# Retention in single precision: raw queries, keys, values, scores and states in place of products of 16-bit parts

## The chip, the cores and the metric

The kernel runs on one core of a Trainium2 chip. The metric is the device time of one execution in microseconds (us). Five engines take part, each with its own instruction stream: TensorE (PE in the profile, its weight loads are PEld), VectorE (DVE), ScalarE (ACT), GpSimd (POOL) and SyncE (SP), which issues most DMAs.

## The reference, cut to what matters

A retention layer feeds two mixture-of-experts layers. Only the retention is touched by the change.

```python
B, H, S, D = 4, 8, 576, 64                     # q, k, v: [B, H, S, D], float32
scores = np.matmul(q, k.transpose(0, 1, 3, 2)) / np.sqrt(D)
gamma = 1.0 - 2.0 ** (-5.0 - np.arange(H))
rel = pos[:, None] - pos[None, :]
Dmat = np.where(rel >= 0, gamma[:, None, None] ** rel, 0.0)
x = np.matmul(scores * Dmat, v)                # then [B*S, H*D] = [2304, 512]
x = moe(x)       # 4 experts, all of them for every token, 512 -> 1024 -> 512
x = moe2(x)      # 8 experts, the best one for each token
```

## The kernel before, in words

**Arithmetic.** Nearly all products are made from 16-bit floats. A float32 operand is split into a high and a low 16-bit part: ACT writes the scaled high part, DVE (`split`, L164 and L165) or POOL writes what is left. A product is then three matmuls (`TERMS`: high by high, high by low, low by high) that add up in the same place in PSUM.

**Retention.** A sequence of 576 positions is cut in 6 chunks of 96 positions (`C`, `NC`), which makes 24 steps for the 4 batches (`NSTEP`). A step handles all 8 heads, two at a time: heads 2p and 2p+1 use the two 64-row or 64-column halves of the array, for p of 0 to 3.

- `at_load(s)`: SP issues two loads, `qkr` (queries and keys, positions along the free dimension) and `vkr` (values and keys, positions on the partitions).
- `at_split(s)`: the parts. ACT and DVE split the queries and keys (`x2`) and the keys by rows (`k2`); POOL multiplies the values by the decay table (`vs`, L199), ACT and POOL split the product (`v2`, L205 and L206).
- `at_a(s)`: PE makes the scores (`sc`, L217, 24 matmuls: contraction 64, 96 weight columns, 96 moving columns). DVE applies the mask (`pf`, L221); ACT, DVE and POOL split the result (`p2`, L222 and L223). If the chunk isn't the last of its sequence, PE makes the chunk's contribution to the state (`u`, L233, 24 matmuls of 64 moving columns), DVE adds the old state, POOL multiplies by the decay (`sn`, L240, L241), and ACT and DVE split the state (`ss`, L243 and L244).
- `at_b(s)`: PE multiplies scores and values (`xo`, L255, 24 matmuls of 96 moving columns) and, unless the chunk is the first, adds the product of the state before and the queries (again L255, 24 matmuls). DVE scales the result (`xf`, L273), ACT and POOL split it into `xc` (L282, L283), the input of the first layer.
- `at_store(s)`: SP writes `xf`, and every fourth step `xc`, to HBM.

**First layer.** Tokens go in 6 blocks of 384 (`NB`), 4 steps to a block. For expert 0 (`e == 0`) the kernel runs `l1_first` (L431) and `l2` (L534) on block after block. Block 0 is made in the prologue: `l1_part(0, 2)` after the first two steps and `l1_part(2, 4)` after the next two, between the splits of the weights (`w_first`). From then on `at_hook`, called four times in a block, issues the store of the step before, `at_a(s+1)`, `at_b(s)`, `at_split(s+2)` and the load of step s+3. So retention runs one block ahead of the first layer, and step 23 is issued in block 4. The experts 1 to 3 use seven products in place of eight (`l1_mixed`, L460); for the first of them the weights are mixed and split in block 5 of expert 0 (`w_hook`). The second layer streams its weights and ends the kernel.

**What sets the order.** Each engine works through its own list in order. The lists follow the source, but the framework's planner may move an instruction ahead of another that it expects to be later; the groups of 24 matmuls of a step are mostly kept whole. SP's queue is in order too: a DMA that waits for its buffer holds up the ones behind it. `at_raw` has three buffers for each of the two loads and `raw_p` five for raw weights. PSUM has two banks for the scores, and one each for `u` and `xo`.

Of the kernel before, what the change touches and what calls it, by code (L numbers as in the profile page):

```python
# [28 lines left out]
KD = DM // 128  # L29
# [10 lines left out]
PROD = {1: (0, 0), 2: (1, 1), 4: (2, 5), 5: (3, 4), 6: (4, 7), 7: (5, 6), 3: (6, 3)}  # L40
TERMS = ((0, 0), (0, 1), (1, 0))

S_QK = 2.0 ** 6
S_V = 2.0 ** 6
S_X = 2.0 ** 9
S_W = 2.0 ** 8
S_X1 = 2.0 ** 11
# [6 lines left out]
def _consts():  # L54
    gamma = 1.0 - 2.0 ** (-5.0 - np.arange(H))
    i = np.arange(C)
    fa, fb = {}, {}
    m = np.zeros((128, C))
    m[:C] = i[:, None] <= i[None, :]
    fa["mask"] = m  # L60
    g = gamma[:, None] ** i[None, :]
    x = np.zeros((128, KD, C))
    for p in range(KD):
        x[:64, p] = g[2 * p]
        x[64:, p] = g[2 * p + 1]
    fa["xtab"] = x * (D ** -0.5) * S_X / (S_QK * S_QK * S_V)
    v = np.zeros((128, H))
    v[:C] = (gamma[None, :] ** -i[:, None]) * S_V
    fa["vtab"] = v
    gt = np.zeros((128, KD))  # L70
    gt[:64], gt[64:] = gamma[0::2] ** C, gamma[1::2] ** C
    fa["gtab"] = gt
    fb["ident"] = np.eye(128)
    fb["first"] = np.broadcast_to(E2 - np.arange(E2), (128, E2))
    s = np.arange(NSLOT)
    at = np.arange(128)[:, None] - 2 * np.arange(2)[None, :]
    fb["tau"] = 128.0 * np.maximum(at // 2, 0)
    fb["even"] = 1 - at % 2
# [12 lines left out]
    return fa, fb, f16  # L91
# [13 lines left out]
def kernel(  # L105
# [19 lines left out]
    pe, act, dve, pool, sp = nc.tensor, nc.scalar, nc.vector, nc.gpsimd, nc.sync  # L125
# [8 lines left out]
    ps = ctx.enter_context(tc.tile_pool(name="ps", bufs=2, space=PSUM))  # L134
    w_a = ctx.enter_context(tc.tile_pool(name="w_a", bufs=1))

    ka = const.tile([128, ca.shape[1]], F32, name="ka")
    kb = const.tile([128, cb.shape[1]], F32, name="kb")
    k16 = const.tile([128, c16.shape[1]], F16, name="k16")

    def cst(name, *dims):
        t, at = (ka, of_a) if name in of_a else (kb, of_b)
        o, n = at[name]
        a = t[:, o:o + n]
        if len(dims) == 2:
            return a.rearrange("p (a b) -> p a b", a=dims[0])
        return a
# [26 lines left out]


    at_ctx = ExitStack()
    at_raw = at_ctx.enter_context(tc.tile_pool(name="at_raw", bufs=3))
    at_2 = at_ctx.enter_context(tc.tile_pool(name="at_2", bufs=2))
    at_1 = at_ctx.enter_context(tc.tile_pool(name="at_1", bufs=2))
    ps_2 = at_ctx.enter_context(tc.tile_pool(name="ps_2", bufs=2, space=PSUM))  # L180
    ps_1 = at_ctx.enter_context(tc.tile_pool(name="ps_1", bufs=1, space=PSUM))
    raws, spl, pm, st = {}, {}, {}, {}
    xcs, xfs = {}, {}

    def at_load(s):
# [6 lines left out]

    def at_split(s):

        a, t = raws.pop(s)
        x2 = at_2.tile([128, 2, 2, KD, C], F16, name="x2")
        split(a, x2[:, 0], x2[:, 1], S_QK)
        vs = at_1.tile([C, H, D], F32, name="vs")
        pool.tensor_tensor(out=vs, in0=t[:, 0], in1=cst("vtab", H, 1)[:C].to_broadcast([C, H, D]), op=ALU.mult)  # L199
        v2 = at_2.tile([C, 2, H, D], F16, name="v2")  # L200
        k2 = None
        if s % NC < NC - 1:
            k2 = at_2.tile([C, 2, H, D], F16, name="k2")
            split(t[:, 1], k2[:, 0], k2[:, 1], S_QK)
        act.activation(out=v2[:, 0], in_=vs, func=ACTF.Copy)  # L205
        pool.tensor_tensor(out=v2[:, 1], in0=vs, in1=v2[:, 0], op=ALU.subtract)  # L206
        spl[s] = x2, v2, k2

    def at_a(s):
        x2, v2, k2 = spl[s]  # L210
        p2 = at_2.tile([C, 2, 2, KD, C], F16, name="p2")
        sc = [ps_2.tile([C, KD, C], F32, tag="sc", name="sc") for _ in range(2)]
        for p in range(KD):
            for n, (x, y) in enumerate(TERMS):
                for r in range(2):
# [12 lines left out]
        u = ps_1.tile([128, KD, D], F32, tag="u", name="u")
        for p in range(KD):
            for n, (x, y) in enumerate(TERMS):  # L230
                for r in range(2):
                    h = 2 * p + r
                    pe.matmul(u[64 * r:64 * r + 64, p], lhsT=k2[:, x, h], rhs=v2[:, y, h], start=(n == 0), stop=(n == 2))  # L233
        sn = at_2.tile([128, KD, D], F32, name="sn")
        gt = cst("gtab", KD, 1).to_broadcast([128, KD, D])
        if c == 0:
            dve.tensor_tensor(out=sn, in0=u, in1=gt, op=ALU.mult)
        else:
            so = st[s - 1][0]
            dve.tensor_tensor(out=sn, in0=u, in1=so, op=ALU.add)  # L240
            pool.tensor_tensor(out=sn, in0=sn, in1=gt, op=ALU.mult)  # L241
        ss = at_2.tile([128, 2, KD, D], F16, name="ss", bufs=3)
        act.activation(out=ss[:, 0], in_=sn, func=ACTF.Copy)  # L243
        dve.tensor_tensor(out=ss[:, 1], in0=sn, in1=ss[:, 0], op=ALU.subtract)  # L244
        st[s] = sn, ss

    def at_b(s):
        x2, v2, k2 = spl.pop(s)
        p2 = pm.pop(s)
        c = s % NC  # L250
        o = ps_1.tile([128, KD, C], F32, tag="xo", name="xo")
# [12 lines left out]
        if c:
            ss = st[s - 1][1]
            for p in range(KD):
                for n, (x, y) in enumerate(TERMS):
                    for r in range(2):
                        row = slice(64 * r, 64 * r + 64)
                        into(r, p, ss[row, x, p], x2[row, y, 0, p], 3 + n, n == 2)  # L270
# [12 lines left out]
        pace["pool"] = pool.tensor_tensor(out=lo, in0=xf, in1=hi, op=ALU.subtract)  # L283
        xfs[s] = xf
# [754 lines left out]
    for e in range(E1):  # L1039
        for b in range(NB):  # L1040
# [161 lines left out]
```

## Time and profile before

| | |
|---|---|
| median of 3 runs | 1085.55 us (1085.05 to 1086.11) |
| the profiled execution's own time | 1084.43 us |
| its span, first to last instruction | 1082.7 us |
| mean granted clock of TensorE | 0.991 |
| PE busy in the span | 1032.4 us (95%) |
| DVE, ACT, POOL busy | 536.4, 414.5, 289.3 us |

The page gives each engine's busy time and the groups of instructions; a matmul's shown duration includes its way through the array, so 24 overlapped matmuls show as one merged entry, and the distance from the start of one group to the start of the next is what they cost. What matters is in which stretch an engine is the one that others wait for.

### The profile page before, as it was taken

The numbers are of one execution on the slowest core, as the hardware profiler recorded it, in microseconds if no ns is written. First come the engines' busy times: TensorE is split into PE (matmuls) and PEld (weight loads), VectorE is DVE, ScalarE is ACT, GpSimd is POOL, SyncE is SP. The second block draws the span as 40 slices with busy tenths as digits, with TensorE's granted clock in tenths as the row PEclk, the third lists the DMA queues.
The fourth block names the chain that finished last, engine by engine and source line by source line (L and its number), as shares of the span: only waits on it lengthen the run. The fifth ranks groups of instructions, "written<-read, shape, count | busy, mean of one in ns | idle before, by whom it ended". The sixth has DMA issues, their size and how long they took to land.

```text
span 1082.7 us, 24429 instructions
## 1 busy us (share of the span) xinstructions
PE 1032.4 (95%) x10355; PEld 713.8 (66%) x10355; DVE 536.4 (50%) x1037; ACT 414.5 (38%) x821; POOL 289.3 (27%) x298
## 2 busy tenths in 40 slices
PE   4799999999899999999999999999999999999996
PEld 3665555555466777777666677776677677777674
DVE  5975555753646555544656654645555511111111
ACT  5654445533524444433444444423333122222121
POOL 5655645634643342000211000000001111212121
PEclk9889999999999999999999999999999999999998
DMA  9564333211534545666687676445525253381692
GB/s 271 184 213 132 116 110 95 90 38 60 188 124 158 191 164 216 250 223 210 230 285 280 236 253 218 159 182 207 198 89 197 88 195 126 135 341 60 253 391 93
DMA packets 51314, 196.27 MB, mean 181 GB/s; under 512 B 6510, under 2 KB 14334, under 8 KB 48896
## 3 DMA queue, kind: packets, MB, share of 16 engines
q1 hardware_dynamic: 40336, 150.72, 39.5%
q0 software_dynamic: 10864, 43.94, 11.9%
q8 instruction: 83, 1.36, 0.5%
q14 instruction: 31, 0.25, 0.1%
HBM read 184.76 MB, written 56.53 MB: 223 GB/s over the span
## 4 chain that ended last, share of the span: by engine, by line
PE 45%; issue 11%; DMA 10%; DVE 6%; ACT 1%; POOL 0%; POOLq 0%; SPq 0%; DVEq 0%; ACTq 0%
PE po L534 25%; DMA out_dram<-y_s,sidxm 8%; PE ph L460 8%; PE pq L460 5%; PE py L460 5%; DVE ht L419 2%; DVE s L165 1%; DMA out_dram<-y_s,sidxe 1%; PE tp L597 1%; PE pg L608 1%; DMA w2d<-s 0%; DVE s L505 0%; DVE w L165 0%; PE p_y L892 0%; ACT ht L418 0%
## 5 line engine op out<-in xcount | busy, mean ns | idle before, releaser
L534 PE MATMUL po<-w,ht 128*128 128x512 f16 x1728 | 384.4, 380 | 7.5 <-DVE ht L419 3.9
L534 PEld LDWEIGHTS <-ht 128*128 128x128 f16 x1728 | 167.2, 98 | 205.3 <-DVE ht L419 7.9
L460 PEld LDWEIGHTS <-w 128*128 128x128 f16 x3024 | 249.2, 98 | 5.6 <-issue 1.2
L460 PE MATMUL ph<-xc,w 128*128 128x192 f16 x1296 | 119.1, 246 | 1.0 <-ACT py L484 1.0
L875 PEld LDWEIGHTS <-lane 128*128 128x128 f16 x1920 | 109.0, 98 | 5.1 <-issue 0.9
L875 PE MATMUL p_h<-x_s,lane 128*128 128x128 f16 x1920 | 111.5, 219 | 0.4 <-issue 0.4
L431 PE MATMUL ph<-xc,w 128*128 128x384 f16 (+1 forms) x672 | 103.6, 312 | 8.5 <-DVE ht L419 4.1
L892 PE MATMUL p_y<-lane,h_s 128*128 128x512 f16 x480 | 107.2, 379 | 0.8 <-DVE h_s L885 0.8
L885 DVE SCALAR_TENSOR_TENSOR h_s<-p_h,h_s 128x512 f16<-128x512 f32 x40 | 27.6, 691 | 159.1 <-ACT h_s L884 159.1
L165 DVE SCALAR_TENSOR_TENSOR s<-sr,s 128x512 f16<-128x512 f32 x128 | 88.7, 735 | 22.7 <-ACT s L164 22.6
L546 DVE SCALAR_TENSOR_TENSOR acc<-po,p_sb,acc 128x512 f32<-128x512 f32 x54 | 40.4, 748 | 117.3 <-PE po L534 117.3
L431 PEld LDWEIGHTS <-w 128*128 128x128 f16 x672 | 65.0, 101 | 42.6 <-issue 10.3
L164 ACT ACTIVATE s<-sr 128x512 f16<-128x512 f32 x128 | 72.4, 623 | 35.9 <-DMA sr<-in_w2s_dram 13.4
L892 PEld LDWEIGHTS <-h_s 128*128 128x128 f16 x480 | 46.6, 98 | 52.6 <-DVE h_s L885 1.2
L460 PE MATMUL pq<-xc,w 128*128 128x192 f16 x864 | 79.8, 246 | 0.0
L460 PE MATMUL py<-xc,w 128*128 128x192 f16 x864 | 77.2, 246 | 0.0
L299 POOL DMA_DIRECT2D xc<-xcd x17 | 12.5, 737 | 206.2 <-PE py L460 206.2
L165 DVE SCALAR_TENSOR_TENSOR w<-wr,w 128x512 f16<-128x512 f32 x82 | 61.7, 767 | 10.7 <-ACT w L164 10.6
L484 ACT ACTIVATE py<-ph 128x384 f32<-128x384 f32 x36 | 17.1, 476 | 130.1 <-PE ph L460 130.1
L372 POOL TENSOR_TENSOR wr<-wr 128x512 f32<-128x512 f32 x24 | 34.8, 1450 | 86.4 <-DVE w L165 85.7
L164 ACT ACTIVATE w<-wr 128x512 f16<-128x512 f32 x82 | 49.3, 623 | 19.1 <-DMA wr<-in_w_dram 13.0
L895 POOL DMA_INDIRECT out_dram<-y_s,sidxm x17 | 17.3, 1017 | 146.8 <-ACT y_s L894 138.2
(168 smaller groups left out, 1093.8 us busy)
## 6 DMA issues: line engine op xcount, KB each, us to landing
lane<-w1d SPq DMA_DIRECT2D x20, 2048.0 KB
lane<-w2d SPq DMA_DIRECT2D x20, 2048.0 KB
wr<-in_w_dram SPq DMA_DIRECT2D x32, 512.0 KB
sr<-in_w1s_dram SPq DMA_DIRECT2D x32, 512.0 KB
w1d<-s SPq DMA_DIRECT2D x32, 512.0 KB
sr<-in_w2s_dram SPq DMA_DIRECT2D x32, 512.0 KB
w2d<-s SPq DMA_DIRECT2D x32, 512.0 KB
xc<-xcd POOLq DMA_DIRECT2D x12, 960.0 KB, 8.8
```

What stands on the lines that cost most here:

```text
L164: act.activation(out=hi, in_=raw, func=ACTF.Copy, scale=scale)
L165: dve.scalar_tensor_tensor(out=lo, in0=raw, scalar=scale, in1=hi, op0=ALU.mult, op1=ALU.subtract)
L372: pace["pool"] = pool.tensor_tensor(out=quarter(k, to), in0=quarter(k, x), in1=quarter(k, y), op=op)
L419: pace["dve"] = dve.scalar_tensor_tensor(out=dst[1], in0=src, scalar=0.0, in1=dst[0], op0=ALU.max, op1=ALU.subtract)
L431: pe.matmul(ph[:, h0:h1], lhsT=w[:, k, u, f * 128:(f + 1) * 128], rhs=x[:, v, k // 2 + 2 * h0:k // 2 + 2 * h1 - 1:2, k % 2], start=(n == 0 ...
L460: pe.matmul(bank[:, i], lhsT=w[:, k, u, f:f + 128], rhs=x[:, v, d, k], start=(first and i == 0 and n == 0), stop=(n == 5), skip_group_chec ...
L534: pe.matmul(po, lhsT=hts[k // 2][:, x, k % 2, i * 128:(i + 1) * 128], rhs=w[:, k, y], start=(n == 0), stop=(n == 3 * KF - 1),)
L546: dve.scalar_tensor_tensor(out=a, in0=po, scalar=p_sb[:, t, e:e + 1], in1=a, op0=ALU.mult, op1=ALU.add)
L875: pe.matmul(ph[:, j], lhsT=w[:, k, x, f * 128:(f + 1) * 128], rhs=xs[:, y, k], start=(n == 0), stop=(n == 3 * KD - 1),)
L885: dve.scalar_tensor_tensor(out=lo, in0=ph, scalar=0.0, in1=hi, op0=ALU.max, op1=ALU.subtract)
L892: pe.matmul(po, lhsT=h[:, a, k], rhs=w[:, k, b], start=(n == 0), stop=(n == 3 * KF - 1))
L895: pool.indirect_dma_start(out=out, out_offset=bass.IndirectOffsetOnAxis(ap=idx[:, s:s + 1], axis=0), in_=y, in_offset=None, bounds_check=N ...
```

## The change

The queries, keys, values, masked scores and states are given to TensorE as float32, as they are. Each group of 24 matmuls becomes 8 (for each head one product in place of three). The mask table carries the decay of the keys (`gamma ** -i` times the triangle, for each head), so the values stay raw. For the state the keys are multiplied by `gamma ** (C - i)` on POOL (`ks`, in float32), where the values were before; the state `sn` is used as it is, and its decayed copy `so` for the next chunk is made on POOL beside it. The splits of `x2`, `k2`, `v2`, `p2` and `ss` are gone. The table `ka` grows from 492 to 1164 columns of float32, and its tile moves from the pool `const` to `at_1`. `at_raw` has four buffers, and the raw tiles are held until `at_b(s)` has read them.

```diff
-    m = np.zeros((128, C))
-    m[:C] = i[:, None] <= i[None, :]
+    m = np.zeros((128, 2, KD, C))
+    for h in range(H):
+        m[:C, h % 2, h // 2] = (i[:, None] <= i[None, :]) * gamma[h] ** -i[:, None]
...
-    v[:C] = (gamma[None, :] ** -i[:, None]) * S_V
-    fa["vtab"] = v
+    v[:C] = gamma[None, :] ** (C - i[:, None])
+    fa["ktab"] = v
...
-    at_raw = at_ctx.enter_context(tc.tile_pool(name="at_raw", bufs=3))
-    at_2 = at_ctx.enter_context(tc.tile_pool(name="at_2", bufs=2))
-    at_1 = at_ctx.enter_context(tc.tile_pool(name="at_1", bufs=2))
+    at_raw = at_ctx.enter_context(tc.tile_pool(name="at_raw", bufs=4))
+    at_1 = at_ctx.enter_context(tc.tile_pool(name="at_1", bufs=3))
...
-        a, t = raws.pop(s)
-        x2 = at_2.tile([128, 2, 2, KD, C], F16, name="x2")
-        split(a, x2[:, 0], x2[:, 1], S_QK)
-        vs = at_1.tile([C, H, D], F32, name="vs")
-        pool.tensor_tensor(out=vs, in0=t[:, 0], in1=cst("vtab", H, 1)[:C].to_broadcast([C, H, D]), op=ALU.mult)
-        v2 = at_2.tile([C, 2, H, D], F16, name="v2")
-        k2 = None
+        ks = None
         if s % NC < NC - 1:
-            k2 = at_2.tile([C, 2, H, D], F16, name="k2")
-            split(t[:, 1], k2[:, 0], k2[:, 1], S_QK)
-        act.activation(out=v2[:, 0], in_=vs, func=ACTF.Copy)
-        pool.tensor_tensor(out=v2[:, 1], in0=vs, in1=v2[:, 0], op=ALU.subtract)
+            ks = at_1.tile([C, H, D], F32, name="ks")
+            pool.tensor_tensor(
+                out=ks, in0=raws[s][1][:, 1], in1=cst("ktab", H, 1)[:C].to_broadcast([C, H, D]), op=ALU.mult
+            )
...
         for p in range(KD):
-            for n, (x, y) in enumerate(TERMS):
-                for r in range(2):
-                    row = slice(64 * r, 64 * r + 64)
-                    pe.matmul(sc[r][:, p], lhsT=x2[row, y, 1, p], rhs=x2[row, x, 0, p], start=(n == 0), stop=(n == 2))
+            for r in range(2):
+                row = slice(64 * r, 64 * r + 64)
+                pe.matmul(sc[r][:, p], lhsT=a[row, 1, p], rhs=a[row, 0, p], start=True, stop=True)
...
-            dve.tensor_tensor(out=pf, in0=sc[r], in1=mask, op=ALU.mult)
-            act.activation(out=p2[:, 0, r], in_=pf, func=ACTF.Copy)
-            (pool if r else dve).tensor_tensor(out=p2[:, 1, r], in0=pf, in1=p2[:, 0, r], op=ALU.subtract)
+            dve.tensor_tensor(out=pf[:, r], in0=sc[r], in1=mask[:, KD * r:KD * r + KD], op=ALU.mult)
...
-                    pe.matmul(u[64 * r:64 * r + 64, p], lhsT=k2[:, x, h], rhs=v2[:, y, h], start=(n == 0), stop=(n == 2))
+                pe.matmul(u[64 * r:64 * r + 64, p], lhsT=ks[:, h], rhs=t[:, 0, h], start=True, stop=True)
...
         if c == 0:
-            dve.tensor_tensor(out=sn, in0=u, in1=gt, op=ALU.mult)
+            act.activation(out=sn, in_=u, func=ACTF.Copy)
         else:
-            so = st[s - 1][0]
-            dve.tensor_tensor(out=sn, in0=u, in1=so, op=ALU.add)
-            pool.tensor_tensor(out=sn, in0=sn, in1=gt, op=ALU.mult)
-        ss = at_2.tile([128, 2, KD, D], F16, name="ss", bufs=3)
-        act.activation(out=ss[:, 0], in_=sn, func=ACTF.Copy)
-        dve.tensor_tensor(out=ss[:, 1], in0=sn, in1=ss[:, 0], op=ALU.subtract)
+            dve.tensor_tensor(out=sn, in0=u, in1=st[s - 1][1], op=ALU.add)
+        so = None
+        if c < NC - 2:
+            so = at_1.tile([128, KD, D], F32, name="so", bufs=2)
+            pool.tensor_tensor(out=so, in0=sn, in1=cst("gtab", KD, 1).to_broadcast([128, KD, D]), op=ALU.mult)
...
+            for r in range(2):
+                into(r, p, t[:, 0, 2 * p + r], pf[:, r, p], True, not c)
+        if c:
+            sn = st[s - 1][0]
+            for p in range(KD):
                 for r in range(2):
...
+                    row = slice(64 * r, 64 * r + 64)
+                    into(r, p, sn[row, p], a[row, 0, p], False, True)
```

## Rows read from the trace of the kernel before

**Rows 1.** The page's busy time: engine, us (share of the span), instructions.

```profile
PE 1032.4 (95%) x10355; PEld 713.8 (66%) x10355; DVE 536.4 (50%) x1037; ACT 414.5 (38%) x821; POOL 289.3 (27%) x298
```

**Rows 2.** Stretches: busy us of PE, PEld, DVE, ACT, POOL; granted clock, DMA share, GB/s.

```profile
0.00:20.00 20.00, 8.12 (x125) 6.43 (x126) 10.77 (x18) 11.34 (x19) 8.85 (x11) 1.00 0.94 276
20.00:40.00 20.00, 12.84 (x222) 9.52 (x222) 16.62 (x24) 11.99 (x24) 14.46 (x13) 0.90 0.88 256
40.00:91.00 51.00, 47.83 (x665) 34.03 (x663) 40.63 (x69) 26.88 (x58) 32.54 (x27) 0.91 0.58 179
91.00:258.00 167.00, 160.49 (x2039) 95.02 (x2039) 93.11 (x141) 72.26 (x140) 79.01 (x68) 1.00 0.29 88
...
300.00:858.00 558.00, 550.65 (x4666) 388.73 (x4663) 308.22 (x681) 225.29 (x465) 85.47 (x111) 1.00 0.55 197
```

**Rows 3.** Waits of PE, 91 to 258 us: us in total, times, longest.

```profile
PE ph L431 <- DVE ht L419: 4.1, 3, 1.8
PE ph L431 <- POOL xc L283: 2.5, 4, 1.0
```

**Rows 4.** Waits of SP's DMA queue, 0 to 91 us, same columns.

```profile
SPq L348 <- DVE w L165: 11.9, 2, 9.5
...
SPq L189 <- DVE x L165: 7.9, 4, 4.1
```

**Rows 5.** Groups on DVE, 0 to 300 us: busy us, mean ns | idle before.

```profile
L165 DVE SCALAR_TENSOR_TENSOR x<-qkr,x 128x768 f16<-128x768 f32 x24 | 30.6, 1274 | 8.9 <-ACT x L164 8.8
...
L165 DVE SCALAR_TENSOR_TENSOR k<-vkr,k 96x512 f16<-96x512 f32 x20 | 23.4, 1171 | 0.6 <-ACT k L164 0.6
...
L244 DVE TENSOR_TENSOR ss<-sn,ss 128x256 f16<-128x256 f32 x20 | 18.6, 929 | 4.9 <-ACT ss L243 4.9
L223 DVE TENSOR_TENSOR p<-pf,p 96x384 f16<-96x384 f32 x24 | 17.5, 727 | 2.6 <-ACT p L222 2.6
```

**Rows 6.** Groups on POOL, the whole span, same columns.

```profile
L206 POOL TENSOR_TENSOR v<-vs,v 96x512 f16<-96x512 f32 x24 | 33.3, 1388 | 30.7 <-ACT v L205 30.7
L223 POOL TENSOR_TENSOR p<-pf,p 96x384 f16<-96x384 f32 x24 | 31.2, 1301 | 15.0 <-ACT p L222 15.0
```

**Rows 7.** DMA, 0 to 40 us: what moved, then issues by size.

```profile
DMA packets 3873, 10.65 MB, mean 266 GB/s; under 512 B 692, under 2 KB 1277, under 8 KB 3869
...
wr<-in_w_dram SPq DMA_DIRECT2D x8, 512.0 KB
qkr<-in_qk_dram SPq DMA_DIRECT2D x7, 384.0 KB
...
ka<-in_ca_dram SPq DMA_DIRECT2D x1, 246.0 KB
```

**Rows 8.** Timeline of PE, one step at 83 us: start us, us.

```profile
83.12 0.74 PE L217 MATMUL sc<-x 64*96 64x96 f16 x24
83.79 0.57 PE L233 MATMUL u<-v,k 96*64 96x64 f16 x24
84.19 0.68 PE L255 MATMUL xo<-p,v 96*64 96x96 f16 x24
84.80 0.70 PE L255 MATMUL xo<-x,ss 64*64 64x96 f16 x24
85.43 5.35 PE L534 MATMUL po<-w,ht 128*128 128x512 f16 x24
90.62 0.33 PE L431 MATMUL ph<-xc,w 128*128 128x384 f16 x1
```

**Rows 9.** Groups on PE, 91 to 258 us: the scores.

```profile
L217 PE MATMUL sc<-x 64*96 64x96 f16 x360 | 11.1, 208 | 0.0
```

**Rows 10.** Timeline of PE, late in the kernel: float32 transposes beside 16-bit matmuls.

```profile
907.51 5.52 PE L875 MATMUL p_h<-x_s,lane 128*128 128x128 f16 x96
912.87 0.61 PE L863 MATMUL p_t<-kb,x_g 128*128 128x128 f32 x4
913.32 5.34 PE L892 MATMUL p_y<-lane,h_s 128*128 128x512 f16 x24
```

More of the change, by code (lines that the diff above doesn't have):

```diff
@@ L41 @@
 TERMS = ((0, 0), (0, 1), (1, 0))
-S_QK = 2.0 ** 6
-S_V = 2.0 ** 6
 S_X = 2.0 ** 9
@@ L65, in _consts @@
         x[64:, p] = g[2 * p + 1]
-    fa["xtab"] = x * (D ** -0.5) * S_X / (S_QK * S_QK * S_V)
+    fa["xtab"] = x * (D ** -0.5) * S_X
     v = np.zeros((128, H))
-    v[:C] = (gamma[None, :] ** -i[:, None]) * S_V
-    fa["vtab"] = v
+    v[:C] = gamma[None, :] ** (C - i[:, None])
+    fa["ktab"] = v
     gt = np.zeros((128, KD))
@@ L135 @@
     w_a = ctx.enter_context(tc.tile_pool(name="w_a", bufs=1))
-    ka = const.tile([128, ca.shape[1]], F32, name="ka")
     kb = const.tile([128, cb.shape[1]], F32, name="kb")
@@ L176 @@
     at_ctx = ExitStack()
-    at_raw = at_ctx.enter_context(tc.tile_pool(name="at_raw", bufs=3))
-    at_2 = at_ctx.enter_context(tc.tile_pool(name="at_2", bufs=2))
-    at_1 = at_ctx.enter_context(tc.tile_pool(name="at_1", bufs=2))
+    at_raw = at_ctx.enter_context(tc.tile_pool(name="at_raw", bufs=4))
+    at_1 = at_ctx.enter_context(tc.tile_pool(name="at_1", bufs=3))
     ps_2 = at_ctx.enter_context(tc.tile_pool(name="ps_2", bufs=2, space=PSUM))
     ps_1 = at_ctx.enter_context(tc.tile_pool(name="ps_1", bufs=1, space=PSUM))
-    raws, spl, pm, st = {}, {}, {}, {}
+    ka = at_1.tile([128, ca.shape[1]], F32, name="ka", bufs=1)
+    raws, pm, st = {}, {}, {}
     xcs, xfs = {}, {}
@@ L193, in at_split @@
     def at_split(s):
-        a, t = raws.pop(s)
-        x2 = at_2.tile([128, 2, 2, KD, C], F16, name="x2")
-        split(a, x2[:, 0], x2[:, 1], S_QK)
-        vs = at_1.tile([C, H, D], F32, name="vs")
-        pool.tensor_tensor(out=vs, in0=t[:, 0], in1=cst("vtab", H, 1)[:C].to_broadcast([C, H, D]), op=ALU.mult)
-        v2 = at_2.tile([C, 2, H, D], F16, name="v2")
-        k2 = None
-        if s % NC < NC - 1:
-            k2 = at_2.tile([C, 2, H, D], F16, name="k2")
-            split(t[:, 1], k2[:, 0], k2[:, 1], S_QK)
-        act.activation(out=v2[:, 0], in_=vs, func=ACTF.Copy)
-        pool.tensor_tensor(out=v2[:, 1], in0=vs, in1=v2[:, 0], op=ALU.subtract)
-        spl[s] = x2, v2, k2
+        ks = None
+        if s % NC < NC - 1:
+            ks = at_1.tile([C, H, D], F32, name="ks")
+            pool.tensor_tensor(
+                out=ks, in0=raws[s][1][:, 1], in1=cst("ktab", H, 1)[:C].to_broadcast([C, H, D]), op=ALU.mult
+            )
+        raws[s] += (ks,)
     def at_a(s):
-        x2, v2, k2 = spl[s]
-        p2 = at_2.tile([C, 2, 2, KD, C], F16, name="p2")
+        a, t, ks = raws[s]
         sc = [ps_2.tile([C, KD, C], F32, tag="sc", name="sc") for _ in range(2)]
         for p in range(KD):
-            for n, (x, y) in enumerate(TERMS):
-                for r in range(2):
-                    row = slice(64 * r, 64 * r + 64)
-                    pe.matmul(sc[r][:, p], lhsT=x2[row, y, 1, p], rhs=x2[row, x, 0, p], start=(n == 0), stop=(n == 2))
-        for r in range(2):
-            pf = at_1.tile([C, KD, C], F32, name="pf")
-            mask = cst("mask", 1, C)[:C].to_broadcast([C, KD, C])
-            dve.tensor_tensor(out=pf, in0=sc[r], in1=mask, op=ALU.mult)
-            act.activation(out=p2[:, 0, r], in_=pf, func=ACTF.Copy)
-            (pool if r else dve).tensor_tensor(out=p2[:, 1, r], in0=pf, in1=p2[:, 0, r], op=ALU.subtract)
-        pm[s] = p2
+            for r in range(2):
+                row = slice(64 * r, 64 * r + 64)
+                pe.matmul(sc[r][:, p], lhsT=a[row, 1, p], rhs=a[row, 0, p], start=True, stop=True)
+        pf = at_1.tile([C, 2, KD, C], F32, name="pf", bufs=2)
+        mask = cst("mask", 2 * KD, C)[:C]
+        for r in range(2):
+            dve.tensor_tensor(out=pf[:, r], in0=sc[r], in1=mask[:, KD * r:KD * r + KD], op=ALU.mult)
+        pm[s] = pf
         c = s % NC
@@ L229, in at_a @@
         for p in range(KD):
-            for n, (x, y) in enumerate(TERMS):
-                for r in range(2):
-                    h = 2 * p + r
-                    pe.matmul(u[64 * r:64 * r + 64, p], lhsT=k2[:, x, h], rhs=v2[:, y, h], start=(n == 0), stop=(n == 2))
-        sn = at_2.tile([128, KD, D], F32, name="sn")
-        gt = cst("gtab", KD, 1).to_broadcast([128, KD, D])
+            for r in range(2):
+                h = 2 * p + r
+                pe.matmul(u[64 * r:64 * r + 64, p], lhsT=ks[:, h], rhs=t[:, 0, h], start=True, stop=True)
@@ L236, in at_a @@
+        sn = at_1.tile([128, KD, D], F32, name="sn")
         if c == 0:
-            dve.tensor_tensor(out=sn, in0=u, in1=gt, op=ALU.mult)
+            act.activation(out=sn, in_=u, func=ACTF.Copy)
         else:
-            so = st[s - 1][0]
-            dve.tensor_tensor(out=sn, in0=u, in1=so, op=ALU.add)
-            pool.tensor_tensor(out=sn, in0=sn, in1=gt, op=ALU.mult)
-        ss = at_2.tile([128, 2, KD, D], F16, name="ss", bufs=3)
-        act.activation(out=ss[:, 0], in_=sn, func=ACTF.Copy)
@@ L244, in at_a @@
-        dve.tensor_tensor(out=ss[:, 1], in0=sn, in1=ss[:, 0], op=ALU.subtract)
-        st[s] = sn, ss
+            dve.tensor_tensor(out=sn, in0=u, in1=st[s - 1][1], op=ALU.add)
[3 more added lines that the diff above has]
+            pool.tensor_tensor(out=so, in0=sn, in1=cst("gtab", KD, 1).to_broadcast([128, KD, D]), op=ALU.mult)
+        st[s] = sn, so
     def at_b(s):
-        x2, v2, k2 = spl.pop(s)
-        p2 = pm.pop(s)
+        a, t, _ = raws.pop(s)
@@ L250, in at_b, with into @@
+        pf = pm.pop(s)
         c = s % NC
         o = ps_1.tile([128, KD, C], F32, tag="xo", name="xo")
-        def into(r, p, lhsT, rhs, n, last):
+        def into(r, p, lhsT, rhs, first, last):
             pe.matmul(
                 o[64 * r:64 * r + 64, p], lhsT=lhsT, rhs=rhs,
-                start=(p == 0 and n == 0), stop=last, skip_group_check=True,
+                start=(p == 0 and first), stop=last, skip_group_check=True,
             )
         for p in range(KD):
-            for n, (x, y) in enumerate(TERMS):
-                for r in range(2):
-                    into(r, p, v2[:, x, 2 * p + r], p2[:, y, r, p], n, not c and n == 2)
@@ L264, in at_b @@
[L264 to L270, printed above, removed]
+            for r in range(2):
+                into(r, p, t[:, 0, 2 * p + r], pf[:, r, p], True, not c)
+        if c:
+            sn = st[s - 1][0]
+            for p in range(KD):
+                for r in range(2):
+                    row = slice(64 * r, 64 * r + 64)
+                    into(r, p, sn[row, p], a[row, 0, p], False, True)
```

## Prediction

> **What bounds the kernel now.** I read the busy times first, then the stretches, then who waits for whom in each stretch, and last the timeline of single steps. PE is busy 95% of the span [rows 1], but that is an average, and retention lives only in the first 258 us. There the table of stretches shows two different limits [rows 2]. From 91 to 258 us PE is busy 160.5 of 167 us at full clock; DVE is busy 56% and POOL 47%. PE waits there for just 4.1 us on DVE and 2.5 us on POOL [rows 3]. So in this stretch only what PE itself executes counts; the splits on the other engines run beside it. From 300 us on PE is busy 550.7 of 558 us [rows 2], and nothing of retention is left, so a shift of the start is carried to the end.
>
> Up to 91 us it is different. In the first 40 us PE is busy 21 us, while the 16 DMA engines are 94% and 88% busy, and from 20 to 40 us DVE is busy 83% and POOL 72% [rows 2]. SP's queue waits there for engines: 9.5 us in one place for a weight buffer that DVE hasn't finished splitting, 7.9 us in all for the splits of queries and keys [rows 4]. So the start is a mixture of transfers and of DVE and POOL work.
>
> How much of it is lost? A step's four groups start 0.67, 0.40, 0.61 and 0.63 us apart, the last one before a group of the first layer [rows 8]: 2.31 us a step. Up to 90.6 us, where block 1 begins [rows 8], the source puts steps 0 to 7 and the scores of step 8: 9 x 0.67 + 8 x 0.40 + 8 x 0.61 + 6 x 0.63 = 17.9 us. Block 0 has 192 matmuls of 192 columns; 128 columns take 5.36/96 = 0.056 us [rows 10] and 512 take 5.19/24 = 0.216 us [rows 8], so 192 about 0.082 us, 15.7 us together. Its second half is 72 x 0.216 = 15.6 us. That makes 49.2 us of PE work; 41.4 us of the 90.6 go into waits and matmuls at half clock (the granted clock is 0.90 and 0.91 from 20 us on [rows 2], a mixture of 2.4 and 1.2 GHz).
>
> **The change, part by part.** *PE, 91 to 258 us.* 360 score matmuls are 15 groups [rows 9]; hooks 8 to 23 add 12 groups of `u`, 16 of scores by values and 14 of states by queries. At the distances of [rows 8] that is 15 x 0.67 + 12 x 0.40 + 16 x 0.61 + 14 x 0.63 = 33.4 us. Each group goes from 24 matmuls in 16 bits to 8 in float32. The trace has no float32 product. The nearest row is the float32 transpose: four take 0.45 us to the next group, 0.112 us each, where a 16-bit matmul of the same 128 x 128 takes 0.056 us [rows 10]. So a float32 operand passes at half rate. A transpose doesn't multiply; I take it that in a product the weights come in two parts as well, each with a half-rate pass. Then one product costs 2 x 2.0 = 4.0 matmuls of 16 bits in place of 3, a factor of 1.34: +11.4 us. This presumes that the two heads of a pair go on overlapping in the two halves of the array, as they do now: a pair of 96 columns takes 0.67/12 = 0.056 us, less than two streams of 96 columns one after the other (2 x 0.042 by [rows 10]). Bounds: below, the factor could be 1 (each distance holds some 0.01 us beyond the stream of 0.04 us, and fewer instructions would save it) or even 0.67, if weights were taken in one part, -11 us. Above, without the overlap the factor is 2.68, +56 us. I take 1.34, since it follows from the nearest row.
>
> The Trainium skill, "FP8 and Floating Point Precision", section TensorE Precision Notes, says that true FP32 takes four passes through the array. By that rule alone the factor is 4/3, the stretch would lose 11.1 us and the sum below would be -7.9 us; the rule speaks against the change, and no run here shows a product yet.
>
> *PE's waits in this stretch* (6.6 us, [rows 3]): in the first layer PE waits for a PSUM bank because DVE is behind, and for POOL's low part of `xc`. DVE loses its four kinds of splits, 30.6 + 23.4 + 18.6 + 17.5 = 90 us over 24 steps, 3.8 us a step [rows 5]; POOL loses 33.3 + 31.2 = 64.5 us [rows 6], and `ks` takes the place of `vs` at the same size. I take -4 us, between 0 and -6.6.
>
> *The start.* SP's order puts before the fourth quarter of the first weights: three steps' loads of 768 KB, four of 512 KB and `ka`, 246 KB [rows 7], 4.7 MB; at 266 GB/s and 2 us of lead they are there at 20 us. `ka` grows to 1164 x 4 x 128 bytes, 0.34 MB more, 1.3 us at the same rate: the table is needed by the first mask and the first `ks`, and this delay is a cost that the change brings; the work beside it (scores from raw operands, without the first split) doesn't depend on it. So the first layer could start at about 22 us. From there PE has 15.7 us of block 0, 15.6 us of its second half and five more steps at 2.31 x 1.34 = 3.1 us: 46.8 us, to 69 us against 90.6, a gain of 22 us. The weights of the second half (9.7 MB up to their last piece, 39 us) are in time for that. Each step still has its chain (scores, mask, values, scaling, split), PE will be at half clock at first, and DVE still has the weights to split. So 22 us is the upper bound; the lower one is 5 us, half of SP's longest wait. I take -15 us, two thirds of the way. The cover that makes the splits free later is not there at the start: this is where taking them away pays.
>
> *At no cost:* the mask without broadcast (same 96 x 384 elements), the copy of the first state on ACT, `so` on POOL (the multiplication moves behind the state that PE reads, so PE waits less). Stores and loads are the same in number. The raw buffers are held until `at_b(s)`, so a load waits for PE and no longer for a split; the fourth buffer keeps the load of step s+3 free of the step being read. If that failed, a load would be late by one step, about 3 us, and PE has the first layer's work before it.
>
> *Sum:* -15 + 11.4 - 4 = -7.6 us. The profiled execution took 1084.43 us, 1.1 us under the median of 1085.55; so 1076.8 by its own time and **1078 us** as a median.
>
> **The rivals.** (1) *Loads of weights stand in the open.* If a product's second part can't be loaded behind its first pass, both loads add up. A float32 load is bounded by the transpose's distance, 0.112 us for 128 columns [rows 10], so 0.084 for 96 and 0.056 for 64. Eight loads for four pairs: 0.67 us in a group of scores and 0.45 us in the others, 15 x 0.67 + 42 x 0.45 = 29 us more in the stretch and 8 us in four steps of the start: -7 + 40.4 - 4, or 1115 us. Against it: `u` uses the same 96 rows for both heads, and its pairs take 0.033 us [rows 8] with a load in each half. The Trainium skill, "TensorE: Matmul & The Clock Gate", section The mechanism, has a load overlap running matmuls only when its row group differs; the distances of `u` speak against so strict a reading.
>
> (2) *The pairs lose their overlap*: factor 2.68, +56 us in the stretch, 12 us in four steps of the start (6.2 in place of 3.1): -3 + 56 - 4, or 1135 us. For it: no row shows float32 in half of the array. This is the case on the other side; every factor above 1.52 is slower, since 33.4 us and four steps of 2.31 us hang on it (7.6/42.6 = 0.18 above 1.34).
>
> (3) *The start doesn't shorten* because the chain of a step or the transfers bind (DMA at 94% [rows 2]): -5 + 11.4 - 4 = +2.4, or 1088 us.
>
> (4) *Float32 costs no more than three 16-bit products*, factor 1, and the start gives 20 us: -20 - 5, or 1061 us.
>
> **How the numbers follow.** About 0.2% (2.2 us) is what a measurement of this kernel can tell from no change. Forecast 0.48 (its own range 1066 to 1087), (4) 0.14, (3) 0.12, (1) 0.14, (2) 0.12. Faster: 0.45 of the forecast and all of (4), 0.59. Within the bound: 0.03 of the forecast and a third of (3), 0.07. Slower: the rest, 0.34. The range reaches from (4) to (1) and leaves out (2) and a little on either side: 1061 to 1115 us.
>
> **What would show it.** In the changed kernel's profile: the first matmul of 384 columns (block 1) near 75 us; the distance of a step's groups near 3.1 us in all, 0.9 for the scores; PE's waits for DVE from block 1 to 4 down to 2 us or less; DVE busy some 90 us less; the stretch from block 1 to block 5 about 7 us longer. A step near 4.8 us would be rival (1), near 6 us rival (2); block 1 after 85 us, rival (3). The prediction is wrong if a float32 product costs over half as much again as three 16-bit ones, or if the start is bound by transfers.

## The result, and the profile after

The changed kernel takes 1068.13 us (median of 4 runs, 1067.48 to 1068.83) beside 1085.3 us for the kernel before on the same chip: a ratio of 0.9844, 95% interval 0.9827 to 0.9861. The profiled execution took 1068.01 us, its span is 1066.2 us, 16.5 us less than before. The direction was forecast, and the time lies in the range; the gain is 17.2 us where 7 to 8 were forecast.

The page's busy times, to be set beside [rows 1]:

```profile
PE 1036.5 (97%) x9651; PEld 719.3 (67%) x9651; DVE 452.4 (42%) x945; ACT 346.5 (33%) x689; POOL 209.8 (20%) x246
```

PE has hardly more to do, DVE 84 us less, POOL 79.5 us less. The same stretches as in [rows 2], with the same columns:

```profile
0.00:20.00 20.00, 12.39 (x167) 10.75 (x167) 7.74 (x15) 6.87 (x12) 7.09 (x11) 1.00 0.93 319
20.00:40.00 20.00, 18.64 (x246) 15.70 (x243) 16.29 (x31) 8.16 (x20) 8.23 (x8) 1.00 0.95 304
40.00:91.00 51.00, 51.00 (x563) 34.52 (x563) 16.56 (x39) 10.89 (x24) 12.32 (x15) 1.00 0.51 165
91.00:258.00 167.00, 167.00 (x1481) 99.38 (x1480) 47.62 (x90) 37.78 (x71) 37.06 (x42) 1.00 0.29 92
```

PE is full from 40 us on, where it had been busy 47.8 of 51 us; DVE falls from 56% to 28% in the last stretch. In the table of PE's waits from 75 to 245 us there is no entry left, where 4.1 and 2.5 us stood [rows 3]. One step of the timeline of PE, to be set beside [rows 8]:

```profile
71.68 6.01 PE L416 MATMUL ph<-xc,w 128*128 128x384 f16 x36
77.62 0.92 PE L209 MATMUL sc<-qkr 64*96 64x96 f32 x16
78.47 0.69 PE L222 MATMUL u<-vkr,ks 96*64 96x64 f32 x16
78.99 0.83 PE L242 MATMUL xo<-pf,vkr 96*64 96x96 f32 x16
79.75 0.88 PE L242 MATMUL xo<-qkr,sn 64*64 64x96 f32 x16
80.56 6.03 PE L416 MATMUL ph<-xc,w 128*128 128x384 f16 x36
...
240.59 15.76 PE L416 MATMUL ph<-xc,w 128*128 128x384 f16 x96
```

Each group of 8 products appears as 16 matmuls, two for a product. The groups stand 0.85, 0.52, 0.76 and 0.81 us apart, 2.94 us in all where it was 2.31. Block 1 begins at 71.68 us (90.62 before, [rows 8]); block 5, the last one of expert 0, at 240.59 us, where the kernel before has it at 258.03:

```profile
258.03 15.76 PE L431 MATMUL ph<-xc,w 128*128 128x384 f16 x96
```

So the start became 18.9 us shorter, blocks 1 to 4 took 168.9 in place of 167.4 us, 1.5 us more, and what follows 825.6 in place of 824.7 us, 0.9 us more: -18.9 + 1.5 + 0.9 = -16.5.

### The profile page after: what moved, and what is told of

Read it like the earlier page. It is cut to its first block, busy times and chain, and to the rows that moved or that the text cites. A ratio compares the mean times of both kernels' runs of the same rounds, so it can differ in the third digit from the quotient of the medians.

```text
span 1066.2 us, 22687 instructions
## 1 busy us (share of the span) xinstructions
PE 1036.5 (97%) x9651; PEld 719.3 (67%) x9651; DVE 452.4 (42%) x945; ACT 346.5 (33%) x689; POOL 209.8 (20%) x246
## 3 DMA queue, kind: packets, MB, share of 16 engines
q8 instruction: 77, 1.26, 0.5%
## 4 chain that ended last, share of the span: by engine, by line
PE 69%; issue 12%; DMA 10%; DVE 6%; POOL 2%; ACT 1%; POOLq 0%; SPq 0%; DVEq 0%; ACTq 0%
PE po L519 33%; PE ph L416 8%; PE ph L445 8%; DMA out_dram<-y_s,sidxm 8%; PE pq L445 5%; PE py L445 5%; PE xo L242 3%; DVE ht L404 2%; PE sc L209 2%; DVE s L164 2%; PE u L222 1%; DMA out_dram<-y_s,sidxe 1%; PE tp L582 1%; PE pg L593 1%; POOL wr L357 1%
## 5 line engine op out<-in xcount | busy, mean ns | idle before, releaser
L416 PE MATMUL ph<-xc,w 128*128 128x384 f16 (+1 forms) x672 | 97.7, 303 | 1.5 <-POOL xc L268 1.2
L404 DVE SCALAR_TENSOR_TENSOR ht<-ph,ht 128x384 f16<-128x384 f32 (+1 forms) x56 | 27.9, 499 | 89.0 <-ACT ht L403 88.9
```

The lines of the kernel that those rows point to most:

```text
L404: pace["dve"] = dve.scalar_tensor_tensor(out=dst[1], in0=src, scalar=0.0, in1=dst[0], op0=ALU.max, op1=ALU.subtract)
L416: pe.matmul(ph[:, h0:h1], lhsT=w[:, k, u, f * 128:(f + 1) * 128], rhs=x[:, v, k // 2 + 2 * h0:k // 2 + 2 * h1 - 1:2, k % 2], start=(n == 0 ...
```

## The experiments

Times are medians; each ratio is to the kernel before, run on the same chip. In each trace I read when block 1 begins (the end of the start) and how long blocks 1 to 4 take.

| run | us | ratio (95% interval) | block 1 at | blocks 1 to 4 |
|---|---|---|---|---|
| before | 1085.3 | | 90.6 | 167.4 |
| changed | 1068.13 | 0.9844 (0.9827 to 0.9861) | 71.7 | 168.9 |
| changed, again | 1067.41 | 0.9844 (0.9831 to 0.9858) | 75.5 | 168.9 |
| all splits, unread | 1085.38 | 1.0015 (1.0004 to 1.0025) | 90.6 | 168.9 |
| DVE's splits, unread | 1074.61 | 0.9905 (0.9888 to 0.9922) | 78.2 | 169.4 |
| POOL's splits, unread | 1073.42 | 0.9904 (0.9888 to 0.9919) | 78.7 | 168.9 |
| before, four raw buffers | 1083.87 | 1.0000 (0.9990 to 1.0009) | 90.8 | 167.4 |
| one half at a time | 1099.79 | 1.0148 (1.0127 to 1.0168) | 85.3 | 187.8 |
| scores twice | 1078.63 | 0.9953 (0.9936 to 0.9969) | 73.2 | 179.1 |
| 16-bit scores from step 9 | 1065.51 | 0.9830 (0.9816 to 0.9845) | 73.0 | 166.2 |
| and 16-bit states | 1063.39 | 0.9801 (0.9788 to 0.9815) | 73.2 | 163.8 |
| the same again | 1062.53 | 0.9805 (0.9791 to 0.9818) | 72.7 | 163.8 |
| all products 16-bit from step 9 | 1061.34 | 0.9791 (0.9778 to 0.9804) | 73.0 | 162.5 |

**What shortened the start?** The first run puts the work of the splits back without a reader:

```diff
+        split(a, x2[:, 0], x2[:, 1], 64.0)
...
+            split(t[:, 1], k2[:, 0], k2[:, 1], 64.0)
+        act.activation(out=v2[:, 0], in_=t[:, 0], func=ACTF.Copy)
+        pool.tensor_tensor(out=v2[:, 1], in0=t[:, 0], in1=v2[:, 0], op=ALU.subtract)
...
+            act.activation(out=p2[:, 0, r], in_=pf[:, r], func=ACTF.Copy)
+            (pool if r else dve).tensor_tensor(out=p2[:, 1, r], in0=pf[:, r], in1=p2[:, 0, r], op=ALU.subtract)
...
+        act.activation(out=ss[:, 0], in_=sn, func=ACTF.Copy)
+        dve.tensor_tensor(out=ss[:, 1], in0=sn, in1=ss[:, 0], op=ALU.subtract)
```

> The changed kernel, with the splits of the kernel before put back on ACT, DVE and POOL at their old places, but read by nobody: TensorE works from the raw operands as in the changed kernel. Theory A, the start got shorter because DVE and POOL were freed: block 1, which begins at 71.7 us in the changed kernel and at 90.6 us before, begins after 82 us here, and the whole is at or above 1078 us. Theory B, it got shorter because TensorE no longer waits for the chain of splits: block 1 begins before 76 us, and the whole stays under 1073 us. In either, TensorE's waits for DVE and POOL between block 1 and block 5 (6.6 us before, none in the changed kernel) come back in part if they are due to DVE and POOL being busy.

```profile
90.57 6.01 PE L432 MATMUL ph<-xc,w 128*128 128x384 f16 x36
```

Block 1 begins at 90.57 us, where it was before the change, although TensorE reads raw operands and waits for no split; the whole is back too, at a ratio of 1.0015. So theory A holds: the time of the start was the splits' occupation of the engines, and not the chain from split to product. One thing isn't separated: in this run and the next two the unread parts have one buffer each, where the kernel before had two (three for `ss`). From 20 to 40 us DVE is busy 98%, as the stretch of this run shows, beside the one of the changed kernel above:

```profile
20.00:40.00 20.00, 13.71 (x145) 10.08 (x143) 19.63 (x25) 12.04 (x25) 16.22 (x12) 0.83 0.82 259
```

Its table of PE's waits in the first 75 us says for whom PE waits now:

```profile
PE xo L258 <- DVE pf L224: 6.6, 5, 3.7
...
PE ph L432 <- DVE w L164: 4.0, 1, 4.0
PE ph L432 <- DVE ht L420: 2.5, 2, 1.4
```

PE waits 13.1 us for things that DVE does late: masks, the weights' splits and the first layer's own split. The last sentence of the expectation missed: PE's waits in blocks 1 to 4 did not come back (below).

Two runs put back one engine's part each, DVE's (with ACT's copies of the same operands, for the scores of both halves) and POOL's (with all copies on ACT):

> As the run with all splits unread, but only those of DVE and their first halves on ACT are put back (queries and keys, keys by rows, one half of the scores, states); POOL's two (values, the other half of the scores) stay out, and so does the copy of the values on ACT. With all of them back, block 1 began at 90.6 us, without any at 71.7. If DVE is what holds the start (98% busy from 20 to 40 us with all back), block 1 begins after 82 us, the whole at or above 1078 us. If it is POOL, block 1 begins before 76 us, under 1073 us.

> The counterpart: POOL's two splits (the low part of the values and of one half of the scores) are put back with all of ACT's copies, read by nobody, and DVE's low parts stay out. If DVE holds the start, block 1 begins before 76 us and the whole is under 1073 us; if POOL does, after 82 us and at or above 1078 us. If both have a share, the two runs' delays add up to about 19 us.

Neither engine alone does it: 6.5 and 7.0 us, 13.5 us together, where about 19 were expected and both at once cost 18.9. These are single profiles; the ratios of the table, from all runs, say the same: 0.6% and 0.6% of the time come back, and 1.7% with both. ACT's copies stand in both runs, so a share of ACT isn't separated. The groups from 0 to 70 us show where at least a part of the rest comes from. The split of the weights on DVE and the low part of the values on POOL, first with all splits back, then with DVE's alone, then with POOL's alone:

```profile
L164 DVE SCALAR_TENSOR_TENSOR w<-wr,w 128x512 f16<-128x512 f32 x16 | 15.8, 1012 | 0.0
...
L209 POOL TENSOR_TENSOR v<-vkr,v 96x512 f16<-96x512 f32 x8 | 14.9, 1857 | 11.8 <-ACT v L208 11.8
```

```profile
L164 DVE SCALAR_TENSOR_TENSOR w<-wr,w 128x512 f16<-128x512 f32 x16 | 12.1, 778 | 0.0
```

```profile
L209 POOL TENSOR_TENSOR v<-vkr,v 96x512 f16<-96x512 f32 x10 | 12.5, 1246 | 13.1 <-ACT v L208 13.0
```

The split of the weights takes 0.78 us on average with DVE's splits alone and 1.01 us with POOL splitting too (0.83 us in the changed kernel, 0.90 us with POOL's splits alone); POOL's instruction goes from 1.25 to 1.86 us. One by one it is clearer: in these traces each split of the weights beside an idle POOL takes 0.67 to 0.69 us, and all longer ones, up to 2.51 us, ran beside work of POOL. The two engines slow each other, so their work costs more together than one by one.

The fourth raw buffer alone, on the kernel before:

```diff
-    at_raw = at_ctx.enter_context(tc.tile_pool(name="at_raw", bufs=3))
+    at_raw = at_ctx.enter_context(tc.tile_pool(name="at_raw", bufs=4))
```

> The kernel before, with four raw buffers in place of three, one part of the change alone. If the queue of SP, which waited for raw buffers and splits in the first 91 us, was what held the start, block 1 begins before 84 us in place of 90.6, and the whole is under 1079 us. If it was the work on DVE and POOL, or the chain of splits, block 1 stays within 2 us of 90.6 and the whole within 2 us of the kernel before.

Nothing: 90.75 us. SP's waits for the splits of queries and keys fell from 7.9 us [rows 4] to 3.1 us, and block 1 didn't move: these waits are not what held the start. SP's wait for a weight buffer (9.5 us, [rows 4]) is as long as before in this run, which says nothing on it.

**What does a float32 product cost?** First the halves of the array out of turn, in all four groups:

```diff
-        for p in range(KD):
-            for r in range(2):
+        for r in range(2):
+            for p in range(KD):
```

> The changed kernel, with each group of float32 products ordered so that the four of one half of the array come first and then the four of the other half, in place of turns. If the two halves overlap only when products take turns (what the forecast presumed), the groups of scores, state, values and states, 0.85, 0.52, 0.77 and 0.81 us apart in the changed kernel, become up to twice as far apart; 42 us more in blocks 1 to 4 and about 10 us more in the start, 1100 to 1122 us. If float32 passes queue one behind the other anyway, nothing changes: 1068 us.

```profile
91.22 1.34 PE L209 MATMUL sc<-qkr 64*96 64x96 f32 x16
92.48 0.79 PE L222 MATMUL u<-vkr,ks 96*64 96x64 f32 x13
93.06 0.30 PE L242 MATMUL xo<-pf,vkr 96*64 96x96 f32 x1
93.11 0.28 PE L222 MATMUL u<-vkr,ks 96*64 96x64 f32 x2
93.19 0.25 PE L242 MATMUL xo<-pf,vkr 96*64 96x96 f32 x1
93.23 0.22 PE L222 MATMUL u<-vkr,ks 96*64 96x64 f32 x1
93.27 1.04 PE L242 MATMUL xo<-pf,vkr 96*64 96x96 f32 x14
94.25 1.26 PE L242 MATMUL xo<-qkr,sn 64*64 64x96 f32 x16
95.44 6.02 PE L416 MATMUL ph<-xc,w 128*128 128x384 f16 x36
```

The scores take 1.26 us in place of 0.85; the step takes 4.22 us (91.22 to 95.44) in place of 2.94, blocks 1 to 4 18.9 us more. The step grows by a factor of 1.43, not by 2, because the halves still run side by side for a part: the lines from 93.06 on show the first products of scores and values between the last ones of the state. The starts of single matmuls, which the timeline merges, show the same for the scores. They form two rows of eight. In each row the starts are 0.085 us apart after a longer first interval, and the second row begins 0.42 us after the first. In turns the two rows begin 0.007 us apart, again with 0.085 us in each. So one part of a product takes 0.085 us for 96 columns in either order, twice the 0.042 us of a 16-bit matmul by [rows 10], and issued in turns the two halves run side by side all the time.

Then the scores twice, from step 9 on:

```diff
-        for p in range(KD):
+        for p in [p for _ in range(2 if s > 8 else 1) for p in range(KD)]:
```

> The changed kernel, with the float32 score products of steps 9 to 23 issued twice into the same place. If TensorE alone limits blocks 1 to 4, all of the added 15 x 0.85 = 12.8 us shows: block 1 unmoved at 71.7 us, block 5 at 253.4 in place of 240.6 us, 1081 us as a whole. If something else still limits there, less than half of it shows, under 1074 us.

```profile
88.68 1.60 PE L209 MATMUL sc<-qkr 64*96 64x96 f32 x32
90.21 0.69 PE L222 MATMUL u<-vkr,ks 96*64 96x64 f32 x16
```

The doubled group takes 1.53 us, so the second half of it 0.68: 15 x 0.68 = 10.2 us. Blocks 1 to 4 became 179.12 - 168.91 = 10.2 us longer. All of the added work shows, so TensorE alone limits this stretch; and the 0.85 us of a group are 16 matmuls of 0.0425 us (0.085 us for a pair of heads, as long as one part alone) and 0.17 us that come once with each group.

**Is float32 right for the later steps?** If blocks 1 to 4 are TensorE's, the three 16-bit products are cheaper there, and the splits may be hidden. From step 9 on, first for the scores alone, then also for states by queries (states split behind `sn`; the scale goes into the multiplications by mask and `xtab`), then for all four:

```diff
+        if s >= 9:
+            x2 = parts[s] = at_2.tile([128, 2, 2, KD, C], F16, name="x2")
+            split(raws[s][0], x2[:, 0], x2[:, 1], 64.0)
...
+                        pe.matmul(sc[r][:, p], lhsT=x2[row, y, 1, p], rhs=x2[row, x, 0, p], start=(n == 0), stop=(n == 2))
...
+                            into(r, p, ss[row, x, p], x2[row, y, 0, p], False, n == 2)
```

> The changed kernel, but from step 9 on the scores alone are again three products of 16-bit parts, with the split of queries and keys on ACT and DVE; all else stays float32. If DVE has the time for it in blocks 1 to 4 (28% busy in the changed kernel), each of 15 groups takes 0.67 in place of 0.85 us: 2.7 us less, block 5 at 237.9 in place of 240.6 us, block 1 unmoved, 1065.4 us. If TensorE's waits for DVE come back (6.6 us in the kernel before), there is no gain: 1068 us or more.

> As the run before, and from step 9 on the products of states and queries are three of 16 bits as well (states split on ACT and DVE). 15 x 0.18 + 13 x 0.18 = 5.0 us less than the changed kernel in blocks 1 to 4 if the splits stay hidden: block 5 at 235.6 us, 1063 us. If the waits come back, 1066 us or more.

Blocks 1 to 4 take 166.16 and 163.82 us: 2.75 and 5.09 us less than 168.91, the forecast 2.7 and 5.0, and PE's table of waits stays empty there. The timeline with 16-bit scores and states has both prices side by side, 0.67 and 0.63 us for the 16-bit groups:

```profile
87.83 0.74 PE L222 MATMUL sc<-x 64*96 64x96 f16 x24
88.50 0.69 PE L235 MATMUL u<-vkr,ks 96*64 96x64 f32 x16
89.02 0.83 PE L259 MATMUL xo<-pf,vkr 96*64 96x96 f32 x16
89.78 0.70 PE L259 MATMUL xo<-x,ss 64*64 64x96 f16 x24
90.41 4.07 PE L441 MATMUL ph<-xc,w 128*128 128x384 f16 x24
```

Block 1 was not unmoved as expected; it began at 73.0 and 73.2 us. To compare on one chip, three versions ran beside each other: all 16-bit from step 9 on, the changed kernel, and scores and states again:

> The changed kernel to step 8, and from step 9 on all four products are three of 16-bit parts again, with all splits (values and decayed keys on ACT and DVE, one half of the scores' low part on POOL). On top of the version with 16-bit scores and states, 15 groups of scores by values take 0.61 in place of 0.77 us and 12 of state contributions 0.40 in place of 0.52: 3.8 us less if the splits stay hidden, 160 us from block 1 to block 5 against 163.8, 1059.5 us as a whole. If DVE's list puts the added splits ahead of what TensorE needs, waits come back as in the kernel before (6.6 us): 1062 us or more, and no gain over the version with 16-bit scores and states.

> The changed kernel itself, beside the mixed versions on the same chip: 1068 us, 168.9 us from block 1 to block 5, with block 1 between 71.7 and 73.2 us, the spread that the runs with the same first eight steps showed.

> The version with 16-bit scores and states from step 9 on, beside the changed kernel on the same chip: 163.8 us from block 1 to block 5, 5.1 us less than the changed kernel, 1063 us.

The mixed version is at 0.9805 where the changed kernel is at 0.9844; the intervals don't touch. All 16-bit gains 1.3 of the expected 3.8 us in blocks 1 to 4, and the waits that were feared are back in part:

```profile
PE ph L472 <- DVE ht L460: 1.6, 2, 1.2
```

At 1061.34 us it has the lowest median of all. Its interval overlaps that of the version with scores and states, but beside it on the same chip each of its five runs (1060.54 to 1061.87 us) is shorter than each of the other's (1062.05 to 1063.89 us). The second profile of the changed kernel was its longest run, 1072.07 us beside 1066.57 to 1068.45 us for the others; its blocks 1 to 4 take 168.9 us again, and block 1 begins at 75.5 us, outside the expected 71.7 to 73.2. The start varies from run to run by up to 4 us, so -18.9 us is a single profile's number; that profile's time, 1068.01 us, is near the median.

## Why the prediction was right in direction and too small

The sum had three terms, and all three were too cautious: the start by 3.9 us, PE's waits by 3.6 us and TensorE's share by 2.3 us. Together that is 9.8 us; with the 0.9 us behind block 5 it is the difference between the forecast -7.6 and the measured -16.5 us.

**What bounds it.** Right: from block 1 on it is TensorE's own work (scores twice: 10.2 of 10.2 us), and up to there DVE and POOL (splits unread: all of the start's gain lost).

**The start: the term that failed most.** Forecast -15 us, between -5 and -22; measured -18.9 us. The cause was the named one, the work of the splits. The step at fault is the choice of two thirds of the way: of the bound of 22 us it kept back 7 for the chain of a step, for matmuls at half clock and for the splits of the weights. Only 3 were needed. In the changed kernel PE waits 4.7 us for masks, `xc` and `ks` before block 1, not at all for the splits of the weights, and runs only its first 14 us at half pace; the bound itself was loose, for the first layer begins at 16.5 us and not at 22. Each engine's relief also sped up the other, which [rows 5] and [rows 6] taken one by one don't say.

The 18.9 us are 13.2 us less idle time of PE (22.2 us before block 1, now 9.0) and 5.7 us less busy time (68.4, now 62.7), although the float32 groups take longer. The clock has a large part in the second. The first four stretches are those of the kernel before in which PE runs at half pace, the fifth is that of the changed kernel:

```profile
0.00:29.20 29.20, 14.29 (x229) 11.50 (x230) 17.98 (x28) 16.84 (x31) 15.77 (x17) 1.00 0.93 264
36.10:42.80 6.70, 4.42 (x28) 3.56 (x28) 4.32 (x9) 3.28 (x8) 5.96 (x6) 0.50 0.64 199
53.20:56.50 3.30, 3.30 (x22) 2.97 (x20) 3.09 (x5) 0.75 (x2) 3.30 (x3) 0.50 0.39 93
70.20:73.50 3.30, 3.30 (x32) 1.79 (x31) 3.30 (x6) 2.27 (x5) 1.45 (x2) 0.50 0.67 189
0.00:14.10 14.10, 8.07 (x94) 7.22 (x95) 3.63 (x8) 4.27 (x7) 4.18 (x9) 1.00 0.90 298
```

The row gives 1.00 at the very start, but the pace there is that of 0.50 (1.2 GHz). The first layer's matmuls show the two paces; 24 of them take 3.67 us, nearly all at 0.50, and 2.14 us at 1.00, both in the kernel before:

```profile
39.69 3.67 PE L431 MATMUL ph<-xc,w 128*128 128x192 f16 x24
...
44.99 2.14 PE L431 MATMUL ph<-xc,w 128*128 128x192 f16 x24
```

From start to start that is 0.160 and 0.083 us. Before 28.7 us it is 0.160 as well, and single scores of one half, 0.045 us apart later, are 0.080 us apart there. So 25.3 us of PE's busy time were at half pace before and 8.1 us in the changed kernel; half of the difference, an estimated 8.6 us, is what the clock gave back. Idle time and half pace go together: in the changed kernel, its second profile, the run with the splits unread and the kernel before, PE is idle 9.0, 11.3, 18.3 and 22.2 us up to block 1, and busy at half pace for 8.1, 10.2, 23.2 and 25.3 us.

**TensorE's share.** Forecast 33.4 x 0.34 = +11.4 us; measured 15 x 0.85 + 12 x 0.52 + 16 x 0.76 + 14 x 0.81 = 42.5 us, +9.1 us, a factor of 1.27. Two parts for a product, each at half rate, and overlap of the halves: all three assumptions hold. The transpose of [rows 10] was the right row for a part's rate (0.112 us for 128 columns, so 0.084 for 96; 0.085 measured for the scores). What was mis-sized is the 16-bit side: by the row of 128 columns a 16-bit matmul takes 0.042 us for 96 columns and 0.028 for 64, but in the kernel before, within one half of the array, the single starts are 0.045 us apart in the scores, 0.0425 in both groups of `xo` and 0.032 in `u`. The float32 parts are 0.085, 0.0825 and 0.058 us apart. Two of these against three of those are a factor of 1.26, 1.29 and 1.21, not 1.34. Both formats also pay a share once a group, 0.17 us for the float32 scores and 0.13 us for the 16-bit ones (0.67 less 12 x 0.045). The rule of the Trainium skill weighed there ("FP8 and Floating Point Precision", TensorE Precision Notes: four passes) agrees with two matmuls a product, each at about half the 16-bit pace (0.085 and 0.045 us); its +11.1 us is near, by 2 us too dear.

**PE's waits.** Forecast -4 of 6.6 us. The stretch grew by 1.5 us while the products grew by 9.1, so 7.6 us went: all of the waits in the table, and 1 us that it doesn't list. But the reason given, that DVE is less busy, isn't needed. With all splits back and unread DVE is busy 82.7 of 168 us from 90 to 258 us (49%, 56% before), and PE doesn't wait there. Before, DVE's list had the next step's split ahead of the first layer's:

```profile
102.12 0.54 DVE L273 TENSOR_TENSOR xf<-xo,ka 128x384 f32<-128x384 f32 x1
102.59 1.44 DVE L165 SCALAR_TENSOR_TENSOR x<-qkr,x 128x768 f16<-128x768 f32 x1
...
103.95 1.01 DVE L419 SCALAR_TENSOR_TENSOR ht<-ph,ht 128x384 f16<-128x384 f32 x2
104.55 2.11 PE L431 MATMUL ph<-xc,w 128*128 128x384 f16 x12 [0.96 <-DVE ht L419]
```

This is the timeline of the kernel before. With the splits unread the list of DVE has the same place in another order:

```profile
100.10 0.55 DVE L274 TENSOR_TENSOR xf<-xo,ka 128x384 f32<-128x384 f32 x1
102.14 0.56 DVE L420 SCALAR_TENSOR_TENSOR ht<-ph,ht 128x384 f16<-128x384 f32 x1 [1.49 <-ACT ht L419]
103.09 1.03 DVE L164 SCALAR_TENSOR_TENSOR k<-vkr,k 96x512 f16<-96x512 f32 x1 [0.39 <-ACT k L163]
```

Here `ht` comes first and the next split after it. But that run differs in a second way: PE's groups are longer, 2.94 us a step in place of 2.31, which leaves DVE more time. Where the splits and the short 16-bit groups are both back (all products 16-bit from step 9), 1.6 us of the waits return. Neither the order alone nor the longer groups alone were tried on the kernel before, so it stays open which of the two took the waits away.

**The rivals.** (1), loads of weights in the open, fell: within one half of the array the scores' parts (96 weight columns) start 0.085 us apart and those of states by queries (64 weight columns) 0.0825, each with a load and 96 moving columns. Half as many weight columns again cost 0.0025 us, where the rival had 0.028. The strict reading of the Trainium skill's rule ("TensorE: Matmul & The Clock Gate", The mechanism), no overlap of a load in the same row group, doesn't fit these distances. (2), no overlap, is a real mechanism: with the halves out of turn a step costs 4.22/2.31 = 1.83 times the 16-bit one, and the kernel is 1.5% slower than before. The halves still overlap for a part in that run, so the full price, a factor of 2.68 and 4.6%, wasn't tested. The 1.83 lies on the other side of the break-even factor of 1.52 named in the forecast; the order of two loops decides the sign. (3) fell: the start shortened by 18.9 us. (4) came nearest to the time and was right about the start (-20), but its factor of 1 is wrong: 1.27.

**What it would show.** Block 1 near 75 us: 71.7. A step near 3.1 us, scores 0.9: 2.94 and 0.85. Waits for DVE down to 2 us: none. DVE 90 us less: 84. Blocks 1 to 4 7 us longer: 1.5, wrong because of the waits and the smaller products.

## What to carry to other kernels

The same splits cost 19 us in the start and, unread, nothing that shows after it (168.9 us with and without them), while the float32 products cost 9 us after it: price a change of number format by the stretch in which each engine limits, and where the limits differ, use both formats (float32 while DVE and POOL hold the kernel up, 16-bit parts where TensorE does: 1061 to 1063 us). Where products use half of the array, issue the two halves in turns. Putting removed work back with no reader tells an engine's occupation from a chain of waits in one run.

## What the runs showed of the hardware that was not expected

- A float32 product appears as two matmuls, each at about half the rate of a 16-bit one: 0.085 us for 96 columns (0.045 in 16 bits), 0.058 us for 64 (0.032). Two halves of the array run side by side, so in turns the distance over both is 0.0425 us; a group of four pairs of scores pays 0.17 us once.
- DVE and POOL slow each other: the same split on DVE takes 0.78 or 1.01 us on average, 0.67 to 0.69 us beside an idle POOL and up to 2.51 us beside a working one; the same subtraction on POOL 1.25 or 1.86 us (spans on POOL are rough). The first layer's split, which reads one of its operands from PSUM, takes 0.34 to 0.36 us in either case.
- In the first stretch of a span the granted clock is given as 1.00, while the pace is that of 0.50: the first scores of the changed kernel take 1.59 us for 16 matmuls, those from 15.19 us on 0.92 us. Within one half the single matmuls start 0.160 us apart, later 0.085 us.

```profile
4.22 1.59 PE L209 MATMUL sc<-qkr 64*96 64x96 f32 x16 [4.22 <-DMA qkr<-in_qk_dram]
...
15.19 0.92 PE L209 MATMUL sc<-qkr 64*96 64x96 f32 x16
```
